# Pooled attention and a tanh-shrink network on one core: three maxima of each pair placed among the products with v, and other work re-timed around them

## The chip, the core and the metric

The kernel runs on one core of a Trainium2 chip. Its time is the device time of one execution in microseconds (us); three executions of the kernel before took 1590.95 to 1592.05 us, median 1591.84. A core has a matrix engine (PE; PEld is its loading of weights), a vector engine (DVE), a scalar engine (ACT), a third elementwise engine (POOL) and an engine that here only issues transfers (SP). They run side by side and wait for one another through semaphores. Matrix products land in PSUM, a small memory that PE writes and DVE and ACT read.

## The reference

The first part is attention with pooled queries (two neighbouring queries are averaged); the second is a two-layer network on its output.

```python
# q, k, v: batch 8, heads 8, sequence 1152, head size 64
q_pool = q.reshape(B, H, S // 2, 2, D).mean(axis=3)          # 576 queries
scores = (1 / sqrt(D)) * q_pool @ k.T
scores = scores - max(scores, axis=-1)
attn = exp(scores); attn = attn / (sum(attn, axis=-1) + 1e-9)
out = attn @ v
x = out.transpose(0, 2, 1, 3).reshape(4608, 512)
h = x @ w_in                                                 # 2048 wide
return (h - tanh(h)) @ w_out
```

## The kernel before

**Pairs, halves and units.** Two heads are worked on at a time, one on each half of the 128 partitions; this is a pair, and there are 32. A pair has two halves of 288 queries: half 0 and half 1. Time in the program is counted in units `u`: 36 to a pair, 18 to a half. At every even unit of a half PE computes the scores of 128 keys for all 288 queries of the half (`scores`, L253), nine such score tiles in all; at the last unit of the half it multiplies the exponentials with v (`pv`, L278, nine key blocks, tile names `p_f,v`), and at the end of half 1 it also adds up the denominators (`z_sums`, L293, names `z,ones`).

**A score tile** takes four products, each for both heads: high part by high part (`ps<-hi`, 288 columns), `lo,hi`, `hi,lo`, and one with `ones_k` that adds minus the row's maximum (`mb`). ACT then writes the exponential (`p_f<-ps`), and POOL sums the exponentials into `z`.

**Maxima.** The maxima of a pair must be known before its scores are computed. So one to two halves ahead, `max_part` (L221) computes rough scores of 128 queries against a third of the keys (`ps<-hi` with 384 columns, in the text M), and DVE takes their maximum (`mx<-ps`). A pair needs 15 such tiles. A table, `spots` (L431), says at which unit each one is issued, counted from the pair's own start, and in which of the lists that are run at a unit: `early` (before the unit's scores), `at` (after them), or `mid` (in the middle of the products with v, L283). The DVE reduction of an M is put into the list `first` of the next unit, ahead of all else there.

**PSUM.** Every score tile, every M, every `pv` and two steps of the work on weights take a place of two banks from a ring of four places (`banks`, L174). The oldest place is handed out; a matrix product that writes into it waits until its last reader has finished. With `place=1` the place is put second to last in the ring and not last, so that the products with v, which were given theirs before, keep the youngest rank.

**Weights.** During attention the weights are turned, block by block, into a high and a low part (`w_block`, L342), one block a pair. `begin` takes a place in PSUM, ACT writes the scaled high half into it, and three DVE operations follow (`ps<-ps`, `w<-ps`, `w<-ps,w`); 18 units later `scale` takes another place. `split` on ACT and a subtraction on POOL (`w_hl`) end the block.

**Columns of x.** For the start of the network four groups of columns of the attention's output are loaded, divided by the denominators, and split into high and low part (L412 to L416, `x0`), by DVE and ACT within the last halves of attention.

Each engine executes its instructions strictly in the order in which the program gives them (`InOrder`). The network after attention (L484 on) is not touched by the change.

Of the kernel before, what the change touches and what calls it, by code (L numbers as in the profile page):

```python
# [10 lines left out]
I32 = mybir.dt.int32  # L11
AF = mybir.ActivationFunctionType
ALU = mybir.AluOpType
# [30 lines left out]
def kernel(  # L44
# [18 lines left out]
    P = 128  # L63
# [3 lines left out]
    KT = S // P  # L67
# [66 lines left out]
    t, n = chunks.pop()  # L134
# [4 lines left out]
    with ExitStack() as actx:  # L139

        sm = actx.enter_context(tc.tile_pool(name="sm", bufs=2))
        op = actx.enter_context(tc.tile_pool(name="op", bufs=1))
# [5 lines left out]
        wp = actx.enter_context(tc.tile_pool(name="wp", bufs=1))  # L148

        ring = [actx.enter_context(tc.tile_pool(name=f"ps_{i}", bufs=1, space=PSUM)) for i in range(4)]  # L150
        ring = ring[1:] + ring[:1]
        pe, act, dve, pool, sp = (InOrder(tc, e) for e in (nc.tensor, nc.scalar, nc.vector, nc.gpsimd, nc.sync))

        HQ = SQ // 2
# [17 lines left out]
        at, first, early, mid = {}, {}, {}, {}  # L172

        def banks(dtype=F32, place=0):  # L174

            ring.insert(len(ring) - 1 - place, ring.pop(0))
            return ring[-1 - place].tile([P, 2, 512], dtype, name="ps")

        end = n_pair * U

        def add(u, f, *args, at=at):
            at.setdefault(u, []).append(lambda: f(*args))
# [95 lines left out]
        def pv(u, hf):  # L278

            w, ps = hf.w, banks()  # L280
            hf.o = ps[:, 0]
            for kt in range(KT):
                if kt == KT // 2 + 1:  # L283
                    run(u, mid)
                for h in range(2):
                    pe.matmul(hf.o[64 * h:64 * h + 64, 0:HQ], w.v[:, h, kt], hf.p[kt][:, h], start=(kt == 0),
                              stop=(kt == KT - 1), tile_position=(0, 64 * h))
            add(u + 1, o_out, w, hf, at=first)
            w.halves.append(hf)
            if hf.n == 1:  # L290
                z_sums(u, w, ps[:, 1])

        def z_sums(u, w, ps):  # L293

            for g in range(3):
                for n in range(2):
                    for h in range(2):
                        r = 64 * h + 32 * n
                        pe.matmul(ps[r:r + 32, 0:HQ], ones, w.halves[n].zs[g][:, h], start=(g == 0), stop=(g == 2),
                                  tile_position=(0, r))  # L300
            add(u + 1, z_out, u + 1, w, ps, at=first)
# [38 lines left out]
        WB = 512  # L340

        def w_block(u, kind, r, c):  # L342

            top = float.fromhex("0x1.dffffep-96")
            raw = wp.tile([P, WB, 2], I32, name="w_raw", bufs=3)
            lo, hi = raw.bitcast(mybir.dt.uint16)[:, :, 1], raw[:, :, 1]
            ts, stt = dve.tensor_scalar, dve.scalar_tensor_tensor
            t = []

            def begin():  # L350

                t[:] = [banks(I32, 1)[:, 0], wp.tile([P, WB], I32, name="w_1", bufs=3)]
                act.activation(whole(t[0]), whole(hi), AF.Copy, scale=2.0 ** -112)

            def scale():
                t[0] = banks(I32, 1)[:, 0]
                ts(t[0], t[1], -0x800000, None, op0=ALU.bitwise_and)

            def split():
                t[0] = wp.tile([P, 2, WB], F32R, name="w_hl", bufs=2)  # L360
                act.activation(t[0][:, 0], whole(t[1]), AF.Copy)

            def whole(x):
                return x.bitcast(F32)

            def store():
                src = t[0].bitcast(F32)
                if kind == 0:
                    f = c // P
                    sp.dma_start(wi_dram[f:f + WB // P, :, :, r].rearrange("f p s m -> p s f m"),  # L370
                                 src.rearrange("p s (f m) -> p s f m", m=P))
                else:
                    sp.dma_start(wo_dram[r, :, :, c:c + WB], src)
            sp.dma_start(raw.rearrange("p n w -> p (n w)"),
                         (w_in, w_out)[kind][r * P:(r + 1) * P, 2 * c:2 * (c + WB)])


            for i, op in ((31, begin),
                          (31, lambda: ts(whole(t[0]), whole(t[0]), -top, top, op0=ALU.max, op1=ALU.min)),
                          (31, lambda: ts(t[1], t[0], -0x80000000, None, op0=ALU.bitwise_and)),  # L380
                          (31, lambda: stt(t[1], t[0], 3, t[1], op0=ALU.logical_shift_left, op1=ALU.bitwise_or)),
                          (49, lambda: t.append(wp.tile([P, WB], I32, name="w_2", bufs=1))),
                          (49, scale),
                          (49, lambda: stt(whole(t[2]), lo, 2.0 ** -36, whole(t[0]), op0=ALU.mult, op1=ALU.mult))):
                add(u + i, op, at=first)

            x = 9 if (kind, r) == (1, NF - 1) else 0
            for i, op in ((50, lambda: pool.tensor_tensor(whole(t[1]), whole(t[1]), whole(t[2]), op=ALU.add)),
                          (66 - x, split),
                          (68 - x, lambda: pool.tensor_tensor(t[0][:, 1], whole(t[1]), whole(t[0][:, 0]), op=ALU.subtract)),  # L390
                          (75 - x, store)):
                add(u + i, op)
# [7 lines left out]
        for i, blk in enumerate(blocks):  # L400

            u = U * i + 5 - (G if i == len(blocks) - 2 else U if i == len(blocks) - 1 else 0)
            add(u, w_block, u, *blk)

        tot = []
        x0 = []
# [5 lines left out]
        add(end - 60, lambda: x0.extend(load_x(lambda: (x_tile(0), x_tile(0)), x0_raw, sp, dve,  # L412
                                               lambda o, x: act.activation(o, x, AF.Copy), *chunks[0])))
        for j in range(NP):
            for i, x in enumerate((0, 22, 27, 30)):
                add(end - 58 + 6 * j + x, lambda i=i, j=j: x0[2][j][i]())  # L416


        wi, wo = [], []
# [6 lines left out]
        for pi in range(n_pair):  # L426
            u = pi * U
            units = dict(load=-86, query_sums=-71, hi=-55, lo=-36, load_v=-30)
            row, step = -19, 3

            spots = [x for half, us in ((-54, (0, 4, 6, 8, 12, 16, 16)), (-36, (2, 4, 6, 12, 16, 16)))  # L431
                     for x in [(early, half)] + [(at, half + i) for i in us]]

            if pi == 0:
                units.update(load=-70, query_sums=-62, hi=-60, lo=-50, load_v=-50)
                spots = [(at, -60 + i) for i in range(15)]
                row, step = -43, 1
                add(u - 51, max_rows, u - 51, 0, 1, 0, 3)
            if pi == 1:
                units.update(load=-104, query_sums=-90, hi=-88, lo=-85)  # L440
                spots = [(early, -36)] + [(at, i - 36) for i in (1, 2, 4, 6, 8, 10, 12, 14, 16, 16)] + 3 * [(mid, -19)] + [(early, -18)]
                row = -15
            if pi == 2:
                spots[:8] = [(at, i - 72) for i in (22, 23, 25, 26, 28, 30, 32, 34)]
            add(u + units["load"], load, pi)
            add(u + units["query_sums"], query_sums, pi, dve if pi < 1 else pool)
            for c in range(0, KQ, SQ):
                add(u + units["hi"], hi_part, pi, c, c + SQ)
            add(u + units["lo"], lo_part, pi, dve if pi > 1 else pool)
            for i, (when, x) in enumerate(spots):  # L450
                add(u + x, max_part, u + x, pi, i // 3, i % 3, int(when is mid), at=when)
            add(u + units["load_v"], load_v, pi)
            add(u + row, max_rows, u + row, pi, step, 0 if pi else 3)

        def run(u, at=at):

            while at.get(u):
                at[u].pop(0)()
# [6 lines left out]
        for u in range(end + 60):  # L465
            run(u, first)
            run(u, early)
            n, r = divmod(u, G)
            if u < end and r % 2 == 0:
                if r == 0:  # L470
                    hf = Half()
                    hf.w, hf.n, hf.p, hf.zs = pairs[n // 2], n % 2, [], []
                    hf.last = 2 * n_pair - 1 - n
                hf.p.append(pf.tile([P, 2, HQ], F32, name="p_f"))
                scores(hf.w, hf.n, r // 2, hf.p[-1])
                if r // 2 in z_groups:
                    add(u + 1, z_part, hf, z_groups[r // 2])
            run(u)
            if u < end and r == G - 1:
                pv(u, hf)  # L480
# [153 lines left out]
```

## Time and profile before

| | us |
|---|---|
| median of three runs | 1591.84 |
| the profiled execution, its own time | 1591.36 |
| its span from first to last instruction | 1589.6 |
| start of the steady pairs to the start of the last half but one | 60.6 to 769.6 |
| start of the network | 792.7 |
| one steady pair: half 1 and the half 0 after it | 13.02 + 11.03 |
| the same, parts ahead of the products with v | 6.91 and 6.52 |

The granted PE clock is full throughout. The profile gives for each instruction when it started and how long it was busy; PE's products overlap their neighbours, so the distance from one start to the next tells more than the busy time. A row of a timeline has the start, the time to the end of the last of the instructions that it merges, the engine, the operation and the tiles (out<-in), and how many; PE's products of the two heads are two instructions, and each product with v counts twice.

### The profile page before, as it was taken

What the parts mean: (1) busy time and instruction counts of PE and PEld (TensorE: products, weight loads), DVE (VectorE), ACT (ScalarE), POOL (GpSimd) and SP (SyncE); (2) the same over time, 40 slices, a digit from 0 to 9 for tenths busy, and PEclk for the clock granted to TensorE, in tenths of its full rate; (3) what the DMA queues carried; (4) which work ended last, traced back from release to release, by engine and by line L of the source; (5) the groups of instructions that cost most, each with busy time, mean ns of one, the idle gap of its engine ahead of it and who ended that gap; (6) DMA issues with size and microseconds to landing.
All of it is one profiled execution on the core that took longest, in us unless ns stands there. A gap on an engine that the chain in (4) does not pass through costs nothing.

```text
span 1589.6 us, 31841 instructions
## 1 busy us (share of the span) xinstructions
PE 1574.3 (99%) x12288; PEld 1232.8 (78%) x12288; DVE 1244.0 (78%) x1731; ACT 1014.6 (64%) x1833; POOL 1013.0 (64%) x756
## 2 busy tenths in 40 slices
PE   7999999999999999999999999999999999999999
PEld 4777777777777777777688888888888888888897
DVE  7888887888878888888787777777777777777786
ACT  3666665665666566566576666666666666666786
POOL 5899999999999999999734333424343333423332
PEclk9999999999999999999999999999999999999999
DMA  4244334343344344345492111011010101110100
GB/s 162 93 133 130 129 139 131 123 147 129 118 146 135 111 143 146 110 130 178 152 348 64 40 40 41 27 40 40 29 39 27 54 27 41 34 34 14 40 24 18
DMA packets 73432, 147.37 MB, mean 93 GB/s; under 512 B 12736, under 2 KB 37440, under 8 KB 73280
## 3 DMA queue, kind: packets, MB, share of 16 engines
q1 hardware_dynamic: 73256, 145.33, 27.8%
q8 instruction: 97, 1.59, 0.4%
q14 instruction: 55, 0.45, 0.1%
q10 hardware_dynamic: 24, 0.00, 0.0%
HBM read 109.20 MB, written 35.95 MB: 91 GB/s over the span
## 4 chain that ended last, share of the span: by engine, by line
PE 97%; DVE 2%; POOL 1%; DMA 0%; ACT 0%; issue 0%; SPq 0%; DVEq 0%; POOLq 0%; ACTq 0%
PE ps L37 47%; PE ps_h L37 25%; PE ps_o L37 25%; DVE mx L37 1%; POOL z L37 0%; DMA q_n<-in_q_dram 0%; ACT p_f L37 0%; DVE kq L37 0%; DMA wo_dram<-w_hl 0%; DVE x L37 0%; POOL w L37 0%; ACT hi L37 0%; DVE w L37 0%; ACT x L37 0%; DVE ps L37 0%
## 5 line engine op out<-in xcount | busy, mean ns | idle before, releaser
L37 DVE TENSOR_REDUCE mx<-ps 128x2 f32<-128x768 f32 x480 | 438.0, 954 | 114.7 <-PE ps L37 113.8
L37 POOL TENSOR_TENSOR g_lo<-g_s,g_hi 128x512 fp32r<-128x512 f32 (+1 forms) x160 | 190.9, 1193 | 481.1 <-ACT g_hi L537 443.5
L37 ACT ACTIVATE p_f<-ps 128x576 f32<-128x576 f32 x576 | 355.7, 652 | 69.0 <-PE ps L37 58.9
L37 PE MATMUL ps_h<-x,wi 128*128 128x512 f32 (+1 forms) x1440 | 318.3, 370 | 0.0
L37 PE MATMUL ps<-hi 64*128 64x288 f32 (+1 forms) x2112 | 307.2, 346 | 10.7 <-ACT hi L37 6.8
L37 PE MATMUL ps_o<-wo,g_hi 128*128 128x512 f32 x1008 | 311.5, 390 | 0.0
L37 POOL TENSOR_TENSOR z<-p_f 128x576 f32<-128x576 f32 x189 | 270.1, 1429 | 40.3 <-ACT p_f L37 40.2
L37 PE MATMUL ps<-p_f,v 128*64 128x288 f32 x2304 | 293.7, 409 | 0.7 <-ACT p_f L37 0.4
L37 PEld LDWEIGHTS ps_h<-x,wi 128*128 128x128 f32 x1440 | 253.1, 188 | 50.5
L37 POOL TENSOR_TENSOR z<-z,p_f 128x576 f32<-128x576 f32 x189 | 269.5, 1426 | 14.8
L37 PEld LDWEIGHTS ps<-hi 64*128 64x128 f32 x2112 | 191.4, 186 | 74.1 <-issue 15.1
L37 PEld LDWEIGHTS ps<-p_f,v 128*64 128x64 f32 x2304 | 159.7, 137 | 114.0 <-ACT p_f L37 11.8
L526 ACT ACTIVATE g_u<-ps_h 128x512 f32<-128x512 f32 (+1 forms) x160 | 88.8, 555 | 235.1 <-PE ps_h L37 232.5
L531 DVE SCALAR_TENSOR_TENSOR ps_w<-g_u,ps_h 128x512 f32<-128x512 f32 (+1 forms) x160 | 103.2, 645 | 148.2 <-ACT g_t L527 147.7
L37 PEld LDWEIGHTS ps_o<-wo,g_hi 128*128 128x128 f32 x1008 | 187.6, 188 | 39.1
L37 PE MATMUL ps_o<-wo,g_lo 128*128 128x512 f32 x504 | 196.2, 389 | 0.0
L37 ACT ACTIVATE o_s<-ps 128x288 f32<-128x288 f32 x64 | 26.3, 411 | 232.4 <-PE ps L37 232.4
L37 PE MATMUL ps<-hi,lo 64*128 64x288 f32 x1152 | 171.0, 293 | 0.0
L37 PE MATMUL ps<-lo,hi 64*128 64x288 f32 x1152 | 170.7, 292 | 0.0
L37 PE MATMUL ps<-mb,ones_k 64*128 64x288 f32 x1152 | 170.4, 292 | 0.0
L536 DVE COPY_PREDICATED g_s<-g_m,g_t 128x512 f32<-128x512 int32 (+1 forms) x160 | 114.2, 714 | 16.7 <-DVE g_s L535 0.5
L534 DVE SCALAR_TENSOR_TENSOR ps_w<-g_s,ps_w 128x512 f32<-128x512 f32 (+1 forms) x160 | 102.9, 643 | 16.6 <-ACT g_m L530 0.5
(69 smaller groups left out, 2267.6 us busy)
## 6 DMA issues: line engine op xcount, KB each, us to landing
q_n<-in_q_dram SPq DMA_DIRECT2D x32, 576.0 KB
kq<-in_k_dram SPq DMA_DIRECT2D x32, 576.0 KB
v<-in_v_dram SPq DMA_DIRECT2D x32, 576.0 KB
x_dram<-o_s SPq DMA_DIRECT2D x32, 288.0 KB
out_dram<-o_s SPq DMA_DIRECT2D x34, 256.0 KB
w_raw<-in_moe_w_in_dram SPq DMA_DIRECT2D x16, 512.0 KB
wi_dram<-w_hl SPq DMA_DIRECT2D x16, 512.0 KB
w_raw<-in_moe_w_out_dram SPq DMA_DIRECT2D x16, 512.0 KB
```

Source lines behind the costliest of these rows:

```text
L37: ins = self.tc.keep_in_program_order(f(*args, **kwargs))
L526: nc.scalar.activation(u, h, AF.Square)
L531: nc.vector.scalar_tensor_tensor(w, u, -P0, h, op0=ALU.add, op1=ALU.mult)
L534: nc.vector.scalar_tensor_tensor(w, s2, P2, w, op0=ALU.add, op1=ALU.mult)
L536: last = nc.vector.copy_predicated(s1, m.bitcast(I32), th).ins
```

## The change

The diff, whole but for context:

```diff
@@ -148,7 +148,7 @@
-        ring = ring[1:] + ring[:1]
+        ring = ring[3:] + ring[:3]
@@ -280,7 +280,7 @@ def pv(u, hf):
-                if kt == KT // 2 + 1:
+                if kt == 2 * KT // 3:
                     run(u, mid)
@@ -349,7 +349,7 @@ def begin():
-                t[:] = [banks(I32, 1)[:, 0], wp.tile([P, WB], I32, name="w_1", bufs=3)]
+                t[:] = [banks(I32)[:, 0], wp.tile([P, WB], I32, name="w_1", bufs=3)]
@@ -375,10 +375,10 @@
-            for i, op in ((31, begin),
-                          (31, lambda: ts(whole(t[0]), whole(t[0]), -top, top, op0=ALU.max, op1=ALU.min)),
-                          (31, lambda: ts(t[1], t[0], -0x80000000, None, op0=ALU.bitwise_and)),
-                          (31, lambda: stt(t[1], t[0], 3, t[1], op0=ALU.logical_shift_left, op1=ALU.bitwise_or)),
+            for i, op in ((30, begin),
+                          (30, lambda: ts(whole(t[0]), whole(t[0]), -top, top, op0=ALU.max, op1=ALU.min)),
+                          (30, lambda: ts(t[1], t[0], -0x80000000, None, op0=ALU.bitwise_and)),
+                          (30, lambda: stt(t[1], t[0], 3, t[1], op0=ALU.logical_shift_left, op1=ALU.bitwise_or)),
@@ -412,8 +412,10 @@
         for j in range(NP):
-            for i, x in enumerate((0, 22, 27, 30)):
-                add(end - 58 + 6 * j + x, lambda i=i, j=j: x0[2][j][i]())
+            x = (-36, -34, -17, -15)[j]
+            for i, x in enumerate((6 * j - 58, x, x + 4, x + 6)):
+                add(end + x, lambda i=i, j=j: x0[2][j][i]())
@@ -428,8 +430,8 @@
-            spots = [x for half, us in ((-54, (0, 4, 6, 8, 12, 16, 16)), (-36, (2, 4, 6, 12, 16, 16)))
-                     for x in [(early, half)] + [(at, half + i) for i in us]]
+            spots = [(early, -54)] + [(at, i - 54) for i in (2, 6, 10, 14)] + 3 * [(mid, -37)]
+            spots += [(at, i - 36) for i in (4, 6, 8, 12, 14, 16, 16)]
```

So in half 1 the eight maxima ahead of the products with v become five, and three come after the sixth of the nine key blocks of those products (29 halves have this). In half 0 there are still seven, but none ahead of the first score tile and none until after the third (30 halves). `begin` of the work on weights moves by one unit, from behind the products with v of half 1 to just ahead of them, and its place in PSUM is now the youngest of the ring when it is taken. The mid point of the products moves by one key block. The ring starts two places further on. At the end of attention the second group of columns of x is divided and split earlier, the third and the fourth group are divided later and split in a row.

On PE, at the end of a half 1, the order before was this (`ps<-hi` with 384 columns is an M, with 288 columns and the three after it a score tile):

```order
L37 MATMUL ps<-mb_124,ones_k 128x288 x2
L37 MATMUL ps<-hi 128x384 x4
L37 MATMUL ps<-p_f,v 64x288 x18
L37 MATMUL ps<-z,ones 32x288 x12
L37 MATMUL ps<-hi 128x384 x2
L37 MATMUL ps<-hi 128x288 x2
```

and it is now:

```order
L37 MATMUL ps<-mb_124,ones_k 128x288 x2
L37 MATMUL ps<-p_f,v 64x288 x12
L37 MATMUL ps<-hi 128x384 x6
L37 MATMUL ps<-p_f,v 64x288 x6
L37 MATMUL ps<-z,ones 32x288 x12
L37 MATMUL ps<-hi 128x288 x2
```

Two M ahead of the products with v and one behind them are gone, and three stand between the twelfth and the thirteenth of the eighteen products; the next half begins with a score tile.

On DVE, over the same half 1 and into the next half 0, the order before was:

```order
L37 TENSOR_REDUCE mx<-ps 128x2 x8
L37 TENSOR_SCALAR ps<-ps 128x512
L37 TENSOR_SCALAR w_11226<-ps 128x512
L37 SCALAR_TENSOR_TENSOR w_11226<-ps,w_11226 128x512
L37 TENSOR_TENSOR lo<-kq,hi 128x1728
L37 TENSOR_REDUCE mx<-ps 128x2 x7
```

and it is now:

```order
L37 TENSOR_REDUCE mx<-ps 128x2 x5
L37 TENSOR_SCALAR ps<-ps 128x512
L37 TENSOR_SCALAR w_11178<-ps 128x512
L37 SCALAR_TENSOR_TENSOR w_11178<-ps,w_11178 128x512
L37 TENSOR_REDUCE mx<-ps 128x2 x3
L37 TENSOR_TENSOR lo<-kq,hi 128x1728
L37 TENSOR_REDUCE mx<-ps 128x2 x7
```

The three operations of the work on weights and `lo`, the low part of a later pair's keys and queries, used to follow each other; three reductions now stand between them.

On DVE in the last two halves of attention the order before was this (`q_n` and `kq` are the buffers in which the columns of x are divided; `ps<-w` is `scale`):

```order
L37 TENSOR_TENSOR kq<-kq 128x512
L37 TENSOR_TENSOR x<-q_n,x 128x512
L37 TENSOR_SCALAR ps<-w_11969 128x512
L37 SCALAR_TENSOR_TENSOR w_12119<-w_raw,ps 128x512
L37 TENSOR_TENSOR kq<-kq 128x512
L37 TENSOR_TENSOR x<-kq,x 128x512 x2
```

and it is now:

```order
L37 TENSOR_TENSOR z<-z,p_f 128x576
L37 TENSOR_SCALAR ps<-w_11929 128x512
L37 SCALAR_TENSOR_TENSOR w_12117<-w_raw,ps 128x512
L37 TENSOR_TENSOR kq<-kq 128x512 x2
L37 TENSOR_TENSOR x<-kq,x 128x512 x2
```

A division and a split of columns of x no longer stand ahead of the last `scale`.

## The prediction

> **What bounds the kernel now.** I read the page first: engines' busy time and the chain that ended last.
>
> ```profile
> PE 1574.3 (99%) x12288; PEld 1232.8 (78%) x12288; DVE 1244.0 (78%) x1731; ACT 1014.6 (64%) x1833; POOL 1013.0 (64%) x756
> PE 97%; DVE 2%; POOL 1%; DMA 0%; ACT 0%; issue 0%; SPq 0%; DVEq 0%; POOLq 0%; ACTq 0%
> ```
>
> PE sets the end, so an edit is worth what it does to the order of PE's work. But 99% does not mean that nothing is left: the timeline of PE over a half 0 (410.55 to 421.58) and the half 1 behind it shows waits inside the busy time.
>
> ```profile
> 410.55 0.58 PE L37 MATMUL ps<-hi 64*128 64x384 f32 x4
> 410.96 0.29 PE L37 MATMUL ps<-lo,hi 64*128 64x288 f32 x2
> ...
> 411.36 0.29 PE L37 MATMUL ps<-hi 64*128 64x288 f32 x2
> ...
> 411.88 0.57 PE L37 MATMUL ps<-hi 64*128 64x384 f32 x4
> ...
> 415.30 0.47 PE L37 MATMUL ps<-hi 64*128 64x384 f32 x4
> 415.61 0.29 PE L37 MATMUL ps<-lo,hi 64*128 64x288 f32 x2
> ...
> 416.00 0.29 PE L37 MATMUL ps<-hi 64*128 64x288 f32 x2
> ...
> 416.53 0.61 PE L37 MATMUL ps<-hi 64*128 64x384 f32 x4
> 417.07 4.59 PE L37 MATMUL ps<-p_f,v 128*64 128x288 f32 x36
> 421.58 0.58 PE L37 MATMUL ps<-hi 64*128 64x384 f32 x4
> ...
> 423.72 0.63 PE L37 MATMUL ps<-hi 64*128 64x384 f32 x4
> 424.19 0.30 PE L37 MATMUL ps<-lo,hi 64*128 64x288 f32 x2
> ...
> 425.29 0.66 PE L37 MATMUL ps<-hi 64*128 64x384 f32 x4
> 425.79 0.29 PE L37 MATMUL ps<-lo,hi 64*128 64x288 f32 x2
> ...
> 428.01 0.55 PE L37 MATMUL ps<-hi 64*128 64x384 f32 x4
> 428.49 4.59 PE L37 MATMUL ps<-p_f,v 128*64 128x288 f32 x36
> ...
> 434.60 0.58 PE L37 MATMUL ps<-hi 64*128 64x384 f32 x4
> ```
>
> A score tile S costs 0.52 us (411.36 to 411.88). M and S together cost 0.70 where nothing is waited for (415.30 to 416.00), so M costs 0.18. From an M to the second product of the S behind it is then 0.31 (415.30 to 415.61); at 423.72 it is 0.47 and at 425.29 it is 0.50, waits of 0.16 and 0.19. The first tile after the products with v takes 0.11 more (410.96 - 410.55 = 0.41), and the entry into them 0.12 (428.49 - 428.01 less two M). Half 0 is 6.52 + 4.51 us, half 1 is 6.91 + 6.11.
>
> What is waited for is a place in the ring of four: a tile needs the place of the tile four before it. The timelines of DVE and ACT give the reader's side.
>
> ```profile
> 415.68 0.96 DVE L37 TENSOR_REDUCE mx<-ps 128x2 f32<-128x768 f32 x1 [0.73 <-PE ps L37]
> 416.90 1.82 DVE L37 TENSOR_REDUCE mx<-ps 128x2 f32<-128x768 f32 x2 [0.26 <-PE ps L37]
> ...
> 430.13 0.69 DVE L37 TENSOR_SCALAR ps<-ps 128x512 f32<-128x512 f32 x1
> ...
> 431.58 0.69 DVE L37 SCALAR_TENSOR_TENSOR w<-ps,w 128x512 int32<-128x512 int32 x1
> 432.19 2.32 DVE L37 TENSOR_TENSOR lo<-kq,hi 128x1728 fp32r<-128x1728 f32 x1
> ```
>
> ```profile
> 410.99 0.41 ACT L37 ACTIVATE z_s<-ps 128x288 f32<-128x288 f32 x1
> 424.85 1.36 ACT L37 ACTIVATE p_f<-ps 128x576 f32<-128x576 f32 x2 [0.27 <-PE ps L37]
> 429.35 0.65 ACT L37 ACTIVATE ps<-w_raw 128x512 f32<-128x512 f32 x1
> 759.21 5.15 ACT L37 ACTIVATE p_f<-ps 128x576 f32<-128x576 f32 x9 [0.39 <-PE ps L37]
> ```
>
> The S that starts in effect at 424.06 (424.19 - 0.13) has its exponential at 424.85, done at 425.50 (0.65), and the S that takes its place goes on at 425.66: 0.79 + 0.65 + 0.16 = **1.60 us from one S to the next use of its place**. The M at 415.30 is read from 415.68 for 0.96; with the same 0.16 that is **1.50 us for an M**. With a queue, a reduction follows the last by 0.86 (1.82 - 0.96), an exponential by 0.56 ((5.15 - 0.65)/8). Four tiles with one M among them last 1.74, so nothing waits; with two M they last 1.40, and about 0.1 to 0.2 us is lost. So DVE's and ACT's delay binds here, more than their load: DVE is idle 0.73 and 0.26 us ahead of the two rows above.
>
> **The change part by part.** With these numbers alone I write down when each tile starts (us from the half's start; P the products with v; a wait in brackets):
>
> ```
> before, half 0: M0 S.29 S.81 M1.33 S1.61(.10) M2.13 S2.45(.14) M2.97 S3.21(.06) S3.73 S4.25
>                 M4.77 S4.95 S5.47 M5.99 M6.27(.10) P6.57
> before, half 1: M0 S.29 M.81 S.99 S1.61(.10) M2.13 S2.48(.17) M3.00 S3.21(.03) M3.73 S4.08(.17)
>                 S4.60 M5.12 S5.37(.07) S5.89 M6.41 M6.62(.03) P6.97(.05)
> after,  half 1: M0 S.29 S.81 M1.33 S1.61(.10) S2.13 M2.65 S2.83 S3.35 M3.87 S4.15(.10) S4.67
>                 M5.19 S5.37 [begin's place] P6.31(.30)
> after,  half 0: S0 S.63 S1.15 M1.67 S1.85 M2.37 S2.83(.28) M3.35 S3.53 S4.05 M4.57 S4.91(.16)
>                 M5.43 S5.69(.08) M6.21 M6.51(.12) P6.94(.13)
> ```
>
> The two of before come out at 6.57 and 6.97 against 6.52 and 6.91 measured, so the method is right to some 0.05 us, and it errs the same way in both kernels.
>
> *Half 1, maxima out of the scores.* 6.97 becomes 6.31. Three M less are 0.54; the waits fall by 0.12 only, for `begin` now takes a place ahead of P without any work of PE, so that P needs the place of the S at 4.67, whose exponential ends too late (0.30).
>
> *Half 1, three M inside the products.* The first pairs do this already:
>
> ```profile
> 30.07 2.65 PE L37 MATMUL ps<-p_f,v 128*64 128x288 f32 x20 [0.26 <-DVE mx L37]
> 32.65 0.79 PE L37 MATMUL ps<-hi 64*128 64x384 f32 x6
> ...
> 35.46 0.57 PE L37 MATMUL ps<-hi 64*128 64x384 f32 x4
> ```
>
> The products take 5.39 us there (30.07 to 35.46), without the M 4.51: 0.88, of which only 0.54 is M; the rest is paid for leaving and re-entering the products. The M should not wait: they come at 6.31 + 2.9 + 0.1, near 9.3 us; `begin` (from 6.7 on ACT, 0.65, then three operations of DVE, 2.14 from 430.13 to 432.27) frees the last place near 9.5, and the third M comes at 9.8. Without that 0.1 of margin each half would lose what `begin` is late. Sum of half 1: -0.66 + 0.88 = **+0.22 us, 29 times: +6.4**.
>
> *Half 0.* 6.57 becomes 6.94: the same tiles, but three S in a row meet an ACT that first copies the results of the half before until 0.85 (row 410.99), and the M stand closer together: **+0.37, 30 times: +11.1**. `lo` may add to this. It starts on DVE when the three new reductions are done, some 12.5 us into half 1 (13.2 long). POOL is then past the sums of the queries and at `w_hl`:
>
> ```profile
> 431.29 1.41 POOL L37 TENSOR_TENSOR z<-z,p_f 128x576 f32<-128x576 f32 x1
> 432.65 3.14 POOL L37 TENSOR_TENSOR kq<-q_n 128x576 f32<-128x576 f32 x1
> 435.75 1.29 POOL L37 TENSOR_TENSOR w_hl<-w,w_hl 128x512 fp32r<-128x512 f32 x1
> ```
>
> `lo` ran from 432.19 to 434.51, and the addition `kq<-q_n` beside it took 3.14 where the equally large one on `z` took 1.41. The two do not overlap: 432.69 to 434.51 is 1.82 for `lo` alone, 434.51 to 435.79 is 1.28 for the addition. If `lo` waits for `w_hl` in the same way (1.2 us), the first reduction of half 0 begins at 2.25, not 2.05, and the list above ends at 7.13: +0.56, 30 times +16.8. I take the middle of both, **+14**.
>
> The Trainium skill (SBUF — State Buffer, section "SBUF: two separate sides") says that DVE and GpSimd share a pair of ports under an exclusive lock, and that whichever starts second is blocked until the other is done. By that rule alone the sum would be the upper one, 1591.4 + 6.4 + 16.8 = 1615; if DVE comes first the lower, 1609.
>
> *Columns of x, `begin` at the end, ring.* In the last half one tile waits for `scale`, which stood behind a division and a split on DVE; but the network waits for POOL's last sum in any case:
>
> ```profile
> 781.55 0.41 PE L37 MATMUL ps<-hi 64*128 64x288 f32 x2 [1.15 <-DVE w L37]
> ...
> 792.67 0.50 PE L37 MATMUL ps_h<-x,w 128*128 128x512 f32 x1
> ```
>
> ```profile
> 781.58 1.67 POOL L37 TENSOR_TENSOR w<-w,w 128x512 f32<-128x512 f32 x1 [0.34 <-DVE w L37]
> ...
> 790.60 1.41 POOL L37 TENSOR_TENSOR z<-z,p_f 128x576 f32<-128x576 f32 x1
> ```
>
> POOL's chain ends at 792.01, and of the 1.15 us only the 0.34 ahead of `w<-w` shortens it: -0.3 to -1.0 (if POOL is also disturbed less). Against that the last but two half has `begin` ahead of P, behind two M: P then waits for the last S, 1.60 less 0.52, 0.36 and 0.12, some +0.5. I take -0.3 for the whole. The ring's start only turns which place comes first; the network's first product waits for PE alone in both orders: 0.
>
> Sum: 6.4 + 14 - 0.3 = 20, on the profiled execution's 1591.4 us (0.5 under the median): **1611 us**, slower by 1.2%.
>
> **The rivals.** *Half 0 pays nothing* (the list above is right for half 1 alone): +6.4, 1598. For it: its seven M are the same number. Against it: four times two M stand a single S apart, before it was twice, and each such place is a window of 1.40 us.
>
> *DVE was the bound, and is relieved: faster.* In half 1 eight reductions are 8 x 0.86 = 6.9 us, just as long as its 6.91 us of scores. If the waits follow that queue, they vanish with five: half 1 6.31 - 0.50 + 0.88 against 6.97, -0.28 times 29; half 0 without its 0.77 against 6.57, -0.40 times 30: 1571. It decides if DVE is never idle between reductions; the idle 0.73 and 0.26 us above, in a half of seven, speak against it, and the wait that ends at 425.66 is for an exponential.
>
> *The parts cancel.* If the waits after are smaller by 0.6 us a pair than listed (half of all of them), the cost of re-entering the products is just paid: 1592.
>
> **How the numbers follow.** Forecast 0.75 (its own range 1604 to 1618: both answers for `lo`, and 0.1 us a pair either way), half 0 free 0.12, cancelling 0.06, faster 0.07. The range of 8 in 10 reaches down to the first rival: 1597 to 1619. A change of 0.2% (3.2 us) is about what a measurement of this kernel can tell from none; slower by more 0.87, within 0.06, faster by more 0.07.
>
> **What would show it.** The products of half 1 should last 7.0 us (6.11 before), the scores ahead of them 6.2 to 6.3 (6.91), those of half 0 6.9 to 7.1 (6.52), with a wait of some 0.28 at the fifth S. `lo` should take about 3 us if it waits for POOL, 1.8 to 2.3 if not. The wait of 1.15 us at 781.55 should be gone. The forecast is wrong if half 0 comes out at or under 6.5, or if P of half 1 starts without a wait.

## The result, and the profile after

The changed kernel takes **1607.95 us** (median of four executions, 1607.56 to 1608.40); the kernel before took 1591.39 (four, 1590.80 to 1592.05). The ratio is 1.0105, 95% interval 1.0093 to 1.0118: slower by about 1%. The profiled execution took 1608.4 us, its span is 1606.6, 17.0 more than before; the granted clock is 1.00 throughout.

The page's line of busy times for the changed kernel:

```profile
PE 1586.4 (99%) x12288; PEld 1229.7 (77%) x12288; DVE 1258.8 (78%) x1731; ACT 1012.9 (63%) x1833; POOL 963.0 (60%) x756
```

The instruction counts of every engine are the same as before; no work was added. PE is still the engine that sets the end, DVE is busy 15 us longer (waiting inside an instruction counts as busy) and POOL 50 us less.

Where the 17.0 us went is read from the busy times by stretches, first of before and then of after (columns: the stretch, its length, then PE, PEld, DVE, ACT and POOL with their instructions, the granted clock, the DMA share and GB/s). The stretches are cut at the same three points of the program: the start of the second pair's half 1, the start of the last half 0 that still has maxima (half 60 of 0 to 63), and the start of the network.

```profile
60.60:747.25 686.65, 686.48 (x7710) 508.67 (x7708) 569.30 (x670) 428.21 (x740) 640.01 (x428) 1.00 0.41 133
747.25:792.67 45.42, 43.93 (x498) 31.98 (x495) 34.46 (x35) 27.77 (x51) 37.90 (x25) 1.00 0.48 155
792.67:1589.60 796.93, 793.13 (x3650) 657.77 (x3648) 591.86 (x962) 531.44 (x998) 295.62 (x268) 1.00 0.16 51
```

```profile
61.66:763.53 701.87, 697.52 (x7710) 505.19 (x7709) 583.75 (x670) 426.49 (x740) 589.73 (x428) 1.00 0.40 130
763.53:809.72 46.19, 44.40 (x499) 32.05 (x495) 36.25 (x36) 27.64 (x51) 37.61 (x24) 1.00 0.46 153
809.72:1606.60 796.88, 793.10 (x3650) 657.83 (x3648) 591.41 (x962) 531.60 (x998) 295.77 (x268) 1.00 0.15 51
```

The 57 steady halves take 15.2 us more, what lies ahead of them 1.1 (61.66 against 60.60), the end of attention 0.8 (each of these two with one half 0 in its new order), and the network nothing. So nearly all of the difference is in the steady pairs, and small pieces stand at their two ends.

The timeline of PE over one steady half 1 (405.98 to 419.20), the half 0 behind it (419.20 to 430.57) and the start of the next half:

```profile
405.98 0.58 PE L37 MATMUL ps<-hi 64*128 64x384 f32 x4
...
411.22 0.47 PE L37 MATMUL ps<-hi 64*128 64x384 f32 x4
...
412.20 3.13 PE L37 MATMUL ps<-p_f,v 128*64 128x288 f32 x24
415.26 0.81 PE L37 MATMUL ps<-hi 64*128 64x384 f32 x6
416.01 1.68 PE L37 MATMUL ps<-p_f,v 128*64 128x288 f32 x12
417.61 1.66 PE L37 MATMUL ps<-z,ones 128*32 128x288 f32 x24
419.20 0.40 PE L37 MATMUL ps<-hi 64*128 64x288 f32 x2
...
421.59 0.67 PE L37 MATMUL ps<-hi 64*128 64x384 f32 x4
422.09 0.30 PE L37 MATMUL ps<-lo,hi 64*128 64x288 f32 x2
...
426.05 4.59 PE L37 MATMUL ps<-p_f,v 128*64 128x288 f32 x36
430.57 0.58 PE L37 MATMUL ps<-hi 64*128 64x384 f32 x4
```

Half 1 has 6.22 us of scores (405.98 to 412.20; 6.91 before) and 7.00 of products (412.20 to 419.20; 6.11 before): 13.22 against 13.02. Half 0 has 6.85 (6.52 before) and 4.52: 11.37 against 11.03. The reduction of the scores in half 1 and the products that are interrupted nearly cancel, as they stand in the prediction; the largest part of the loss is in half 0, whose tiles are the same number as before.

DVE and POOL around the start of that half 0:

```profile
414.89 0.69 DVE L37 SCALAR_TENSOR_TENSOR w<-ps,w 128x512 int32<-128x512 int32 x1
415.75 2.69 DVE L37 TENSOR_REDUCE mx<-ps 128x2 f32<-128x768 f32 x3 [0.17 <-PE ps L37]
418.35 3.02 DVE L37 TENSOR_TENSOR lo<-kq,hi 128x1728 fp32r<-128x1728 f32 x1
421.30 1.81 DVE L37 TENSOR_REDUCE mx<-ps 128x2 f32<-128x768 f32 x2
```

```profile
416.93 1.40 POOL L37 TENSOR_TENSOR kq<-q_n 128x576 f32<-128x576 f32 x1
418.29 1.27 POOL L37 TENSOR_TENSOR w_hl<-w,w_hl 128x512 fp32r<-128x512 f32 x1
```

`kq<-q_n` on POOL takes 1.40 us where it took 3.14, since `lo` no longer runs beside it. `lo` now runs beside `w_hl` and takes 3.02: POOL's subtraction ends at 419.56, and 421.37 is 1.81 later, the length of `lo` alone in the prediction.

### The profile page after: what moved, and what is told of

Read it like the earlier page. It is cut to its first block, busy times and chain, and to the rows that moved or that the text cites. A ratio compares the mean times of both kernels' runs of the same rounds, so it can differ in the third digit from the quotient of the medians.

```text
span 1606.6 us, 31862 instructions
## 1 busy us (share of the span) xinstructions
PE 1586.4 (99%) x12288; PEld 1229.7 (77%) x12288; DVE 1258.8 (78%) x1731; ACT 1012.9 (63%) x1833; POOL 963.0 (60%) x756
## 4 chain that ended last, share of the span: by engine, by line
PE 51%; ACT 0%; DVE 0%; issue 0%; ACTq 0%
PE ps_h L37 25%; PE ps_o L37 25%; PE ps L37 2%; ACT p_f L37 0%; ACT x L37 0%; DVE w L37 0%; ACT w_hl L37 0%; ACT x L571 0%; ACT o_s L37 0%; ACT z_s L37 0%; ACTq L37 0%
## 5 line engine op out<-in xcount | busy, mean ns | idle before, releaser
L37 PE MATMUL ps<-p_f,v 128*64 128x288 f32 x2304 | 300.1, 410 | 5.7 <-DVE mx L37 0.7
```

What stands on the lines that cost most here:

```text
L37: ins = self.tc.keep_in_program_order(f(*args, **kwargs))
```

## The experiments

Each experiment changes a line or two of before or of the changed kernel. This table has the distances between the starts of PE's work, from the middle of each profile (scores + products, in us), and `lo`'s median duration; time is the median, with the number of executions.

| kernel | half 1 | half 0 | `lo` | time |
|---|---|---|---|---|
| before | 6.91 + 6.11 | 6.52 + 4.51 | 2.32 | 1591.4 (4) |
| after | 6.22 + 7.00 | 6.85 + 4.52 | 3.03 | 1607.95 (4) |
| before, half 0's new order alone | 6.91 + 6.11 | 6.84 + 4.52 | 2.31 | 1600.4 (4) |
| after, half 0's old order | 6.22 + 6.99 | 8.09 + 4.51 | 3.03 | 1642.5 (1) |
| after, a second break in the products | 6.22 + 7.33 | 6.84 + 4.52 | 2.07 | 1616.9 (1) |
| before, `begin` ahead of P alone | 7.41 + 6.11 | 6.68 + 4.52 | 2.56 | 1611.3 (1) |
| after, `begin` in the middle of P | 6.04 + 7.70 | 6.84 + 4.52 | 2.74 | 1621.9 (4) |
| after, `begin` at P's start, ahead of `split` | 6.04 + 7.18 | 6.84 + 4.52 | 1.95 | 1606.9 (1) |
| the same, three M one key block later | 6.04 + 6.98 | 7.03 + 4.52 | 2.71 | 1607.5 (4) |
| the same, `w_hl` later on POOL | 6.04 + 6.98 | 6.84 + 4.52 | 1.95 | 1602.9 (4) |
| before, columns of x alone | 6.91 + 6.11 | 6.52 + 4.52 | 2.32 | 1590.5 (11) |

**The theory**, as the prediction has it: what PE waits for is a place in the ring of four, 1.60 us from one score tile to the next use of its place and 1.50 for an M; so the order of S and M alone sets the length of a half, and a break in the products has a fixed price. **Rivals**: half 0's new order costs nothing by itself, and the loss comes from DVE's and POOL's operations that meet there (`lo`); the price of the break is a price for each M; `begin`, not the M, makes half 1 what it is.

### Half 0's order alone

```diff
 # before
-            spots = [... (-36, (2, 4, 6, 12, 16, 16)) ... for x in [(early, half)] + [(at, half + i) for i in us]]
+            spots = [... (-36, (4, 6, 8, 12, 14, 16, 16)) ... for x in ([(early, half)] if half == -54 else []) + ...]
```

> The kernel before, with the changed table for half 0 alone (seven M, none ahead of the fourth tile); half 1 keeps its eight, begin its unit. Theory of the ring (the order of M and S costs by itself): half 0 goes from 11.03 to some 11.4 us as in the changed kernel, 30 times 0.34 to 0.37, so 1602 us. Rival (half 0 only got slower because lo is late on DVE behind the three new reductions): lo is early here, half 0 stays at 11.0 to 11.1, 1591 to 1593 us.

Measured: 1600.4 us against 1591.17, ratio 1.0056 (1.0041 to 1.0071). Two rows of PE and one of DVE from this run, in its half 0 (415.10 to 426.45):

```profile
415.10 0.40 PE L37 MATMUL ps<-hi 64*128 64x288 f32 x2
...
421.94 4.59 PE L37 MATMUL ps<-p_f,v 128*64 128x288 f32 x36
```

```profile
417.16 2.69 DVE L37 TENSOR_REDUCE mx<-ps 128x2 f32<-128x768 f32 x3 [2.16 <-PE ps L37]
```

The scores take 6.84 us, as in the changed kernel, although `lo` is here early and DVE idle for 2.16 us before the first reduction. Every tile of this half starts within 0.02 us of its time in the changed kernel. So the order alone costs 0.33 us a half (30 halves: 10 us), and `lo` is not needed to explain any of it. Half 1 is unchanged, 13.02. That half 0 pays nothing for its new order falls.

That the wait is for the place of the tile four before can be read from the trace. In the changed kernel the fifth S of half 0 goes on at 421.96 (its second product at 422.09, less 0.13). The tile four before it is the third S, and this is its exponential on ACT:

```profile
421.14 0.66 ACT L37 ACTIVATE p_f<-ps 128x576 f32<-128x576 f32 x1
```

It ends at 421.80, so PE goes on 0.16 us later, the figure of the prediction. The four other S that are late in this half (3.47, 4.06, 4.93 and 5.67 us into it) also go on 0.16 or 0.17 after the last reader of their place, two of them after an exponential and two after a reduction; in the run of the order alone it is the same.

### The old order of half 0 in the changed kernel

```diff
 # after
-            spots += [(at, i - 36) for i in (4, 6, 8, 12, 14, 16, 16)]
+            spots += [(early, -36)] + [(at, i - 36) for i in (2, 4, 6, 12, 16, 16)]
```

> The changed kernel with the table of before for half 0 (an M ahead of the first tile). Theory: lo runs on DVE until some 2.1 us into half 0 and the first reduction behind it, so the fifth tile waits 1.7 us for the place of the first M: scores of half 0 8.1 to 8.2 us, half 0 12.6 to 12.7, 30 times 1.3: 1647 us. Rival (DVE has slack and the late lo is harmless): half 0 back at 11.0, 1598 us.

Measured: 1642.5 us; scores of half 0 8.09. One row of PE and two of DVE:

```profile
438.93 0.40 PE L37 MATMUL ps<-hi 64*128 64x288 f32 x2 [1.43 <-DVE mx L37]
```

```profile
434.97 3.04 DVE L37 TENSOR_TENSOR lo<-kq,hi 128x1728 fp32r<-128x1728 f32 x1
437.93 1.81 DVE L37 TENSOR_REDUCE mx<-ps 128x2 f32<-128x768 f32 x2
```

Here the half begins with an M (at 435.83), whose reduction stands behind `lo` and starts 2.10 us later; the tile that takes its place then waits 1.43 us. So the two parts of the change belong together: with three reductions and `lo` at the end of half 1, a half 0 that begins with an M is 1.24 us longer than in the changed kernel, whose order avoids this and costs 0.33. The old order with `lo` kept apart from `w_hl` was not run.

### A second break in the products

```diff
 # after: def pv(u, hf)
+                if kt == 3 and len(mid.get(u, [])) == 3 and u > 36:
+                    mid[u].pop(0)()
                 if kt == 2 * KT // 3:
                     run(u, mid)
```

> The changed kernel, but the first of the three M comes after the third key block of the products, the other two after the sixth: the same matrix work with one more break. Theory: what is paid is the leaving and re-entering, 0.34 us a break beside the M's own 0.18: products of half 1 7.34 us (were 7.00), 29 times: 1618 us. Rival (an M inside the products costs 0.30 each, break or not): 7.00, 1608 us.

Measured: 1616.9 us; products 7.33, where the same three M in one place gave 7.00. PE in this run:

```profile
416.15 1.68 PE L37 MATMUL ps<-p_f,v 128*64 128x288 f32 x12
417.76 0.44 PE L37 MATMUL ps<-hi 64*128 64x384 f32 x2
418.13 1.68 PE L37 MATMUL ps<-p_f,v 128*64 128x288 f32 x12
419.74 0.62 PE L37 MATMUL ps<-hi 64*128 64x384 f32 x4
```

One M as a break lasts 0.37 us (417.76 to 418.13), and the products ahead of it 1.61 for three key blocks, 1.50 without a break (4.51 / 3). Of these 0.48 us the M is 0.18, so the break itself is 0.30 here; by the length of the whole products it is 0.33 a half, with no M added. The price is for leaving and re-entering the products, not for each M: the matrix work is the same in both runs.

### `begin` ahead of the products, alone

```diff
 # before
-            for i, op in ((31, begin), (31, ...), (31, ...), (31, ...),
+            for i, op in ((30, begin), (30, ...), (30, ...), (30, ...),
-                t[:] = [banks(I32, 1)[:, 0], ...]
+                t[:] = [banks(I32)[:, 0], ...]
```

> The kernel before, with begin of the work on weights one unit earlier and its place taken ahead of the products' (no other part of the change). Theory: the products of half 1 then need the place of the last S but behind it only two M and begin, which has no PE work: by the same list they wait 0.6 us, scores of half 1 7.5 us (6.9 before), 31 times 0.55: 1608 us. Rival (a place that is taken without PE work costs PE nothing): 1591 us.

Measured: 1611.3 us; scores of half 1 7.41, 0.50 more than before. The wait stands at the products:

```profile
413.82 4.59 PE L37 MATMUL ps<-p_f,v 128*64 128x288 f32 x36 [0.44 <-ACT p_f L37]
```

`begin` takes a place without work of PE, and the products then need the place of the last S, where they needed that of the S before it. Behind two M, as here, that costs 0.50; behind one M and an S, as in the changed kernel, 0.18 (below). Half 0 is 0.16 longer as well, and DVE tells why. These are `lo` and the reductions behind it in this run (half 0 starts at 419.93), and below them the first reduction of half 0 before (410.55):

```profile
418.14 2.56 DVE L37 TENSOR_TENSOR lo<-kq,hi 128x1728 fp32r<-128x1728 f32 x1
420.62 3.84 DVE L37 TENSOR_REDUCE mx<-ps 128x2 f32<-128x768 f32 x4
```

```profile
411.03 0.96 DVE L37 TENSOR_REDUCE mx<-ps 128x2 f32<-128x768 f32 x1 [0.56 <-PE ps L37]
```

With `begin`'s operations ahead of the last reductions of half 1, `lo` comes later, and the first reduction of half 0 starts right behind it, 0.69 us into the half where it was 0.48. The fifth tile, which takes the place of that first M, goes on at 1.79 us where it did at 1.62, and so the half is longer.

### `begin` inside the products: a miss, and its cause

```diff
 # after: begin and its three DVE operations go into a list pre, and begin's place=1
                 if kt == 2 * KT // 3:
+                    run(u, pre)
                     run(u, mid)
```

> The changed kernel, but begin and its three DVE operations are issued inside the products, ahead of the three M, so that the products have their place before begin takes one. Theory: the wait of 0.30 ahead of the products goes (scores of half 1 5.9 us, was 6.2); the third M then comes 0.3 earlier than the place that begin frees and waits 0.1 to 0.2, products 7.0 to 7.2. Half 1 13.0 to 13.1, 29 times 0.1 to 0.2: 1602 to 1605 us. Rival (the products wait for the last exponentials whatever place they get): scores stay at 6.2, 1608 us.

Measured: 1621.9 us (ratio 1.0190, 1.0173 to 1.0207), where some 1604 was expected. The scores of half 1 did fall, from 6.22 to 6.04: the wait of the products for the place is gone, and it was 0.18, not 0.30. But the products rose by 0.70. PE, DVE and ACT of this run:

```profile
447.40 0.62 PE L37 MATMUL ps<-hi 64*128 64x384 f32 x4
448.46 0.44 PE L37 MATMUL ps<-hi 64*128 64x384 f32 x2 [0.45 <-DVE w L37]
```

```profile
447.72 0.69 DVE L37 SCALAR_TENSOR_TENSOR w<-ps,w 128x512 int32<-128x512 int32 x1
```

```profile
445.05 0.62 ACT L37 ACTIVATE w_hl<-w 128x512 fp32r<-128x512 f32 x1
445.57 0.65 ACT L37 ACTIVATE ps<-w_raw 128x512 f32<-128x512 f32 x1
```

The third M needs `begin`'s place, which the last DVE operation on it sets free (447.72 + 0.69 = 448.41). `begin` on ACT now stands behind `split` (`w_hl<-w`), which in the changed kernel it stands ahead of: 0.52 us later. That the third M waits in the products is the point at which the prediction gave a margin of 0.1 us.

Two more runs tell whether that is the whole cause:

```diff
 # after, with begin's place=1: begin and its DVE operations run when the products have taken their place, then split
             hf.o = ps[:, 0]
+            run(u, pre)
+            run(u, post)
```

> The changed kernel with begin and its three DVE operations issued at the start of the products of half 1, right behind the place of the products, and with split on ACT (the copy w_hl) issued behind begin, no longer ahead of it. Theory (the run with begin in the middle of the products lost because split, 0.52 us of ACT, stood ahead of begin, and the third M then waited up to 0.78 for begin's place): begin is 0.52 earlier, the third M waits about 0.26, scores of half 1 stay at 6.04, products go from 7.70 to 7.2, half 1 13.2, whole 1607 to 1609. Rival (the place is late through DVE's own queue, not through ACT): products stay near 7.7 and the whole near 1622.

Measured: 1606.9 us, products 7.18, half 1 13.22, as the theory has it. ACT, and the three M on PE:

```profile
411.60 0.65 ACT L37 ACTIVATE ps<-w_raw 128x512 f32<-128x512 f32 x1
412.17 0.63 ACT L37 ACTIVATE w_hl<-w 128x512 fp32r<-128x512 f32 x1
```

```profile
413.94 0.98 PE L37 MATMUL ps<-hi 64*128 64x384 f32 x6
```

The three M last 0.98 where they lasted 0.81 without a wait: 0.17 is lost for the third, what the scores gained to 0.01. Against the changed kernel the half is neither longer nor shorter. With the three M one key block later as well (`if kt == 7`):

> As the kernel with begin ahead of split at the start of the products, and the three M after the seventh key block of the products instead of the sixth, so 0.48 us later. Theory (only the wait for begin's place is left beside the price of the break itself): no M waits, products 6.9 to 7.0, scores 6.0, half 1 12.9 to 13.0, 0.2 to 0.3 under the changed kernel, whole 1600 to 1602. Rival (the place is late through DVE's queue): a wait of 0.3 or more remains and the whole is 1608 or more. A second rival, that three M nearer to the end of the products delay the reductions and so half 0: half 0 longer than 11.37 by 0.3 or more, whole 1610.

Measured: 1607.5 us. Half 1 came out as the theory said, 6.04 + 6.98 = 13.02, the same as before the change. But half 0 grew by 0.19: that is the second rival, though less than the 0.3 that it named, and the two nearly cancel. DVE and POOL at the start of that half 0 (418.74):

```profile
418.40 2.70 DVE L37 TENSOR_TENSOR lo<-kq,hi 128x1728 fp32r<-128x1728 f32 x1
421.02 2.67 DVE L37 TENSOR_REDUCE mx<-ps 128x2 f32<-128x768 f32 x3
```

```profile
418.01 1.27 POOL L37 TENSOR_TENSOR w_hl<-w,w_hl 128x512 fp32r<-128x512 f32 x1
```

`lo` ends 1.82 us after `w_hl` (419.28 to 421.10), and the first reduction starts 2.28 us into the half. In the changed kernel it was 2.10 (421.30 - 419.20), and there half 0 lost nothing. The last experiment takes POOL's subtraction out of the way:

```diff
 # the kernel above
-                          (68 - x, lambda: pool.tensor_tensor(t[0][:, 1], ..., op=ALU.subtract)),
+                          (68 - x if x else 73, lambda: pool.tensor_tensor(t[0][:, 1], ..., op=ALU.subtract)),
```

> As the kernel with begin at the start of the products and the three M after the seventh key block (1607.5; half 1 13.02, half 0 11.55, lo on DVE 2.70 us, which ends 1.82 after POOL's w_hl), with the subtraction w_hl on POOL issued two sums later, behind the first two sums z of half 0 instead of ahead of them. Theory (lo is stretched because it waits for w_hl on POOL, and half 0 pays for it only where lo ends later than some 2.1 us into half 0): lo takes 1.8 to 1.9, the first reduction of half 0 waits for PE again and starts 2.05 into it, half 0 is 11.35, half 1 stays 13.02, whole 1601 to 1602. Rival (lo is long for a reason of its own, or the next operation of POOL does the same to it): lo stays at 2.5 or more, half 0 at 11.5 to 11.6, whole 1607 to 1608.

Measured: 1602.9 us (1602.56 to 1603.97), half 0 11.36, half 1 13.02. DVE, POOL, and one row of PE from the end of attention:

```profile
415.45 1.95 DVE L37 TENSOR_TENSOR lo<-kq,hi 128x1728 fp32r<-128x1728 f32 x1
417.86 2.69 DVE L37 TENSOR_REDUCE mx<-ps 128x2 f32<-128x768 f32 x3 [0.46 <-PE ps L37]
```

```profile
420.82 1.29 POOL L37 TENSOR_TENSOR w_hl<-w,w_hl 128x512 fp32r<-128x512 f32 x1
```

```profile
802.93 0.68 PE L37 MATMUL ps<-z,ones 128*32 128x288 f32 x4 [1.18 <-POOL z L37]
```

`lo` takes 1.95, DVE is idle again ahead of the first reduction (which waits for PE), and half 0 is back at 11.36. The steady pairs are 5.6 us shorter in all. Of that, 1.3 is given back in the last half of attention (14.70 us, 13.36 in the run before this one), where the sums on POOL now stand behind a later `w_hl`, and the products that add up the denominators wait for them. With the waits for `begin`'s place and behind `w_hl` removed, a pair still takes 24.38 us against 24.05: the 0.33 of half 0's order remain.

The last half was already 0.9 us longer in all four kernels that move `begin` behind the products' place (13.35 or 13.36 without the later `w_hl`, 12.47 in the changed kernel). The network's first product waits in them, as in this row of the last run:

```profile
804.42 0.96 PE L37 MATMUL ps_h<-x,w 128*128 128x512 f32 x3 [0.81 <-ACT z_s L37]
```

`z_s` is ACT's copy out of the place in PSUM that the last products took. In the changed kernel the network does not wait for it. The prediction put the ring's start at nothing, which holds for the two kernels that it compared; that the order of places decides this wait is a likely reading, and no run tests it.

### The columns of x alone

```diff
 # before
-            for i, x in enumerate((0, 22, 27, 30)):
-                add(end - 58 + 6 * j + x, ...)
+            x = (-36, -34, -17, -15)[j]
+            for i, x in enumerate((6 * j - 58, x, x + 4, x + 6)):
+                add(end + x, ...)
```

> The kernel before with the changed units of the columns of x alone. Theory: the wait of 1.15 us in the last half goes and that half takes 12.5 us (13.6 before), but the half ahead of it takes 10.0 (9.5 before), since two splits of columns then stand close together on ACT between its exponentials: -0.6 us, 1591.0 us. Rival (POOL's chain of sums alone sets the start of the network): 0 to -0.3 us.

Measured: 1590.54 us (11 executions) against 1591.07 (15), ratio 0.9996, interval 0.9987 to 1.0005: not to be told from no change by time. In the trace it can be seen. The network starts here:

```profile
791.74 1.45 PE L37 MATMUL ps_h<-x,w 128*128 128x512 f32 x5
```

That is 0.93 earlier than before; of it the last two halves are 0.6 (22.49 us from 769.25 to 791.74 here, 23.09 from 769.58 before), and the rest lies at the start of the program, which the change does not touch. The last half is 1.1 shorter, since the wait for `scale` is gone, and the last but one 0.5 longer, since two splits of x stand on ACT nearer to each other, one exponential apart where it was three. The expected -0.6 stands in this trace, but the times can't tell it from nothing. No kernel of these runs is measurably faster than the one before.

## Why the prediction came out as it did

The prediction was 1611 us with 0.87 on slower; 1608 was measured. Its terms against the trace:

| term | predicted | measured |
|---|---|---|
| half 1, scores | 6.97 to 6.31 in the lists: -0.66 | 6.91 to 6.22: -0.69 |
| half 1, three M in the products | +0.88 | +0.89 |
| half 1, 29 times | +6.4 | +5.8 |
| half 0, order alone | +0.37 | +0.33 |
| half 0, `lo` beside `w_hl` | 0 to +0.19, middle taken | 0.0 |
| half 0, 30 times | +14 | +10.0 |
| end of attention (`begin`, columns of x) | -0.3 | +0.4 |
| first pair and what lies ahead | 0 | +0.8 |
| sum | +20 | +17.0 |

**Half 1 was right.** The price of the break was read from the first pairs, which already interrupted their products, and it held for all. The scores fell as listed, though with two errors that cancel in part: the wait of the products for `begin`'s place was 0.18 (from the runs that move `begin` behind it), not 0.30, and the list was already 0.06 too long for the kernel before (6.97 against 6.91). Without that wait the scores are 6.04, where the list has 6.31 less 0.30.

**Half 0's order was right**, and it is the largest part of the loss. The wait at the fifth S was named as 0.28; the trace has 0.50 from the M at 421.59 to the second product at 422.09, 0.31 without a wait: 0.19. The list was 0.1 us too long in all, and 0.05 too long already for the kernel before; up to the last M it holds to 0.1 us at every tile.

**The mis-sized term is `lo` in half 0.** The mechanism stood in the prediction and took place: `lo` waited for `w_hl` and took 3.02 us. The Trainium skill (SBUF — State Buffer, section "SBUF: two separate sides") says that of a DVE operation with two SBUF inputs and a GpSimd operation that reads SBUF, the one that starts second is blocked until the other is done. The rows agree: `w_hl` starts at 418.29, `lo` at 418.35, and `lo` ends 1.81 after `w_hl`. But the price did not follow. The step that failed is "the first reduction of half 0 begins at 2.25, not 2.05": it began at 2.10, since `lo` started 12.37 us into half 1 and not 12.5. DVE would have been idle until 2.05 in any case, so nearly the whole wait lay in idle time. The run with the three M a key block later shows the priced case: the reduction starts at 2.28 there, and the half is longer by 0.19, the figure of the prediction; the run with `w_hl` later takes it away again. So of the two answers the lower one applied, and the middle between them was 0.1 us a half too high, 3 us of the 1611.

**The ends of attention were off by more than their size.** The columns of x gave -0.6, inside the bounds that were named. `begin`'s place cost more than the +0.5 that was put against it:

```profile
44.19 1.19 PE L37 MATMUL ps<-p_f,v 128*64 128x288 f32 x8 [0.42 <-DVE mx L37]
...
770.67 1.68 PE L37 MATMUL ps<-p_f,v 128*64 128x288 f32 x12 [0.36 <-ACT p_f L37]
...
777.20 0.40 PE L37 MATMUL ps<-hi 64*128 64x288 f32 x2 [0.65 <-DVE w L37]
```

The second row is the wait that was foreseen (+0.31). The first is a wait of the same kind in the half 1 of the first pair, whose maxima the change leaves alone and which was not looked at (14.76 us against 14.07). The third, in half 61, is a score tile that takes the place of `scale` (12.02 against 11.29). Both stand in the run with `begin` ahead of the products alone (14.57 and 12.03), and half 61 is back at 11.36 where `begin` comes behind them: they belong to `begin`'s place and not to the maxima. Of the 0.69 of the first pair this is 0.50. The other 0.19 is still there where `begin` stands behind the products and the three M after the sixth key block (14.26). It comes from the moved mid point: the three M in the products ahead of that half are one key block later, and its third score tile goes on 0.2 us later, 0.16 after the last of their reductions.

The two ends together came out 1.5 us above the prediction and so offset part of what `lo` was put too high. The hit does not hang on that: with the ends as predicted the sum is +15.5, 1607 us, still inside 1604 to 1618.

**The rivals.** Half 0 for nothing fell with the run of its order alone, +9.2 us by itself. That DVE was the bound fell too: by it half 1 would have lost 0.28, and it became 0.20 longer; and half 0 grew with DVE idle for 2.16 us at its start (in the run of its order alone). That the parts cancel holds for half 1 alone, to 0.2 us.

## What to carry to other kernels

When tiles go round a small ring of PSUM places, write the start time of each tile down from three numbers of the trace (a tile's cost, the time from it to the next use of its place, and the reader's spacing in a queue); this gave both halves to 0.1 us, while the engines' busy times say nothing (99% before and after). Moving work from a crowded stretch into a long run of products is not free: here each break costs 0.33 us beside the work itself, nearly twice what one maximum costs (0.18). Three maxima moved out of the scores gave 0.69 us there and cost 0.89 in the products; with `begin`'s place taken behind the products and the M one key block later they gave 0.87 and cost 0.87, so three maxima just pay for one break. An operation that is stretched by a wait should be priced only from the moment at which something else needs its engine: `lo` with 3.02 us cost nothing where the next reduction started 2.10 us into the half, and with 2.70 it cost 0.19 where that was 2.28.

## What the runs showed of the hardware that was not expected

A change of PE between the products with v (128 rows on 64 columns) and maximum tiles (64 rows on 128 columns) shows nearly the same price at each key block where it was tried: 0.35 us after the sixth (0.89 less three M of 0.18), 0.33 after the seventh (0.87 less the same), and 0.33 for a second break after the third, for leaving and re-entering together.

`lo` has a length of its own of 1.95 us when nothing runs on POOL beside it (the run with `w_hl` later). Where a POOL operation is running when it starts, it ends 1.81 to 1.84 after that operation in nearly every pair, however early it started: after `z<-z,p_f` in the kernel before (2.32 in all), after `w_hl` in the changed one (3.02), and after `w_hl` with the M later (2.70). So its end is set there by POOL's order, not by its own start. Four times in all these runs it started within 0.03 us of the end of `kq<-q_n`, and was held by the next operation, `w_hl`, as well. It goes the other way round too: where `lo` starts first, in the run with a second break, `w_hl` takes 3.01 us in place of 1.27.
